# Seven products in two widths, and block sums from DRAM scratch, in three passes of a token-mixing MLP

## The chip, the cores and the metric

The kernel runs on one core of a Trainium2 chip. A core has a matrix engine (TensorE, in the profile PE, its weight loads PEld), a vector engine (VectorE, DVE), an activation engine (ScalarE, ACT), a general engine (GpSimd, POOL), and a sequencer that mostly issues DMAs (SyncE, SP). Sixteen DMA engines move data between DRAM and the core's memory (SBUF); matmul results lie in eight banks of PSUM. The metric is the device time in microseconds (us) of one execution, the median of several runs.

## The reference, cut to what matters

```python
h = x + A(layernorm(x))            # linear attention with softmax features, 32 heads
h2 = h + B(layernorm(h))           # token-mixing MLP

# B, with S = 2048 tokens, D = 512 channels, F = 1792 hidden units
u = einsum("bsd,sf->bdf", layernorm(h), w1) + b1
u = gelu(u)
y = einsum("bdf,fs->bds", u, w2) + b2
return y.transpose(0, 2, 1)
```

Everything is fp32. A matmul operand is split into a high part in the matrix engine's fast fp32 form and the rest, its low part; a product is then high x high + high x low + low x high, three matmuls.

## The kernel before

The core works through four stages. The projections of attention come first. Then come 18 turns (`for it in range(NT + 2)`, L840) of late attention: turn `it` transposes query features of token tile `it`, computes the attention output of tile `it - 1` on the matrix engine, adds the residual (`s_h`, L637), normalizes tile `it - 2` (`s_moments`, `s_rstd`, `s_hn`), and fills the matrix engine's remaining time with the first two of the MLP's seven passes over `w1` (`fill`, L703). Third come the other five passes over `w1` (letters `KINDS = "vuuuv"`, steps 0 to 39, eight steps a pass), and last the 56 steps (8 x 7) over `w2`. `step(n)` (L1143) runs one step; in `w1` a step takes two token tiles, in a pass of two times 128 hidden units.

A pass marked `v` multiplies plainly. A pass marked `u` multiplies 2 x 2 blocks by seven products instead of eight (a Strassen-Winograd scheme): P1 to P7 (L983) each pair one of seven weight blocks with one of seven activation blocks of 256 columns. Four blocks of `w1` are loaded (index 1 to 4); of the seven weight blocks used, three are plain (2, 3, 4) and four are sums (0, 1, 5, 6). `w_sums` (L793) makes the sums with four VectorE additions per pair of steps: index 0 = 3 + 1, 5 = 0 + 2, 6 = 4 + 5, and last 1 = 1 + 2. `w_parts` (L807) then splits a step's seven blocks, high part on ScalarE (L66), low part on VectorE (L67). Steps over `w2` use the same scheme.

`narrow` (L985) is a product of three matmuls of 256 columns. `wide` (L991) puts the high and the low part of the activations side by side in one bank: one matmul of 512 columns (high weights times both) and one of 256 (low weights times high); the two halves of the bank are added later. Before the change the `u` passes use only `narrow` (`products`, L1009, four banks a pass, from `four_banks`, L1006: one pass takes four banks of pool `ps_b`, the next two of `ps_f` and two of `ps_q`), while the steps over `w2` (`wide_step`, L1041) already take P2 to P5 with `wide` and P1, P6, P7 with `narrow`, in six banks. After a `u` pass `firsts` and `u_out` (L1015, L1024) add the products to four blocks of u, on one ScalarE copy and five VectorE operations; two steps later comes the gelu.

Raw weights come by SP in groups of two steps: `load_raw(g)` (L762) issues two DMAs of 256 KB, into one half of one of two buffers that hold four steps each (`BLOCK`).

In late attention the MLP's weights for `fill` come by SP too (`stream`, L686, tile `wraw`), one or two DMAs of 256 KB a turn, issued behind the store of a finished h tile (`out<-h`, L642) and the load of a coming one (`h<-in_x`, L635). In the same turn ScalarE makes the high part (`his`, L677), then VectorE the low part (`flush`, L684, tile `whl`), and `fill` multiplies with them from the next turn on.

The order on PE, DVE, ACT, POOL and SP from the end of the projections on is the order of the code (a manual schedule); each engine runs its own queue in order and waits on semaphores. `later`, `at` and `PENDING` place work at a step number; `U_ADDS` gives the steps at which POOL issues accumulating DMAs (`nc.gpsimd.dma_start(..., accum_op=ALU.add)`, L951), which add one tile to another on the way. An accumulating DMA is always issued by POOL here (queue q0 in the profile), plain ones by SP (q1).

Of the kernel before, what the change touches and what calls it, by code (L numbers as in the profile page):

```python
# [9 lines left out]
F32 = mybir.dt.float32  # L10
# [7 lines left out]
P = 128  # L18
# [14 lines left out]
UR = 6  # L33
PLAIN = 2
KINDS = "vuuuv"
HD = D // 2
NP = NF // 2
WARM = 9
# [1 line left out]


@with_exitstack
def block_kernel(ctx: ExitStack, tc: tile.TileContext, x, xT, wT, phic, wo, w1, b1, w2, b2,
                 kvmask, ident_in, out):
    nc = tc.nc

# [56 lines left out]
    ps_k = a1.enter_context(tc.tile_pool(name="ps_k", bufs=2, space=PSUM))  # L103
    ps_v = a1.enter_context(tc.tile_pool(name="ps_v", bufs=2, space=PSUM))
    kvp = ps_kv.tile([P, 4, 64], F32, name="kvp")

    X, XH, EQ, PK, VS, SQ, PS, W = {}, {}, {}, {}, {}, {}, {}, {}

# [373 lines left out]
    for j in range(KD):  # L482
        WO[j] = w2p.tile([P, D], F32, name=f"wo{j}")
        nc.sync.dma_start(WO[j], wo[j * P:(j + 1) * P, :])
    az = aq.enter_context(tc.tile_pool(name="az", bufs=2, side="right", reuse_waits="tile"))
    EZ = {}

# [305 lines left out]
    def w_sums(g):  # L793

        if 2 * g >= len(STEPS) or STEPS[2 * g][0] == "v":
            return
        plain = STEPS[2 * g][0] == "y"
        raw = BLOCK[g // 2 % 2] if plain else RAW[g]
        added = ADDED(2 * g)
        if not added:  # L800
            nc.vector.tensor_add(raw[:, :, 0], raw[:, :, 3], raw[:, :, 1])
        nc.vector.tensor_add(raw[:, :, 5], raw[:, :, 0], raw[:, :, 2])
        nc.vector.tensor_add(raw[:, :, 6], raw[:, :, 4], raw[:, :, 5])
        if not added:
            nc.vector.tensor_add(raw[:, :, 1], raw[:, :, 1], raw[:, :, 2])  # L805

    def w_parts(n):  # L807
        if n >= len(STEPS):
            return
        if n >= Y0 and (n - Y0) % 6 < 3:  # L810
            PARTS[n] = [big.tile([P, 7, P], F32R, name="wp", tag="big") for _ in range(2)]
        else:
            t = ws[n % 3].tile([P, 2, 7, P], F32R, name="wp")
            PARTS[n] = t[:, 0], t[:, 1]
        k = slice(1, 5) if STEPS[n][0] == "v" else slice(0, 7)
        split(PARTS[n][0][:, k], PARTS[n][1][:, k], RAW[n // 2][:, n % 2, k], nc.vector)

    CB_FIRST = (0, 1, 2, 3)
    U_ADDS = {0: (5, 7, 9), 1: (6, 8, 10), 2: (11, 13, 15), 3: (19, 21, 23), 4: (28, 30, 32), 5: (34, 35.5, 37)}
    HELD = (44,)  # L820
    T_WORK = {5: 39.5}
    U_WORK = {0: 26, 1: 28, 2: 30, 3: 32, 4: 34, 5: 38, 6: 41}
# [13 lines left out]
        return (ws[3] if j in CB_FIRST else cbb if j == 4 else hp).tile([P, 4, 2, HD], F32R, name=f"cb{j}")  # L836

    NB, DQ, DL = {}, [], []

    for it in range(NT + 2):  # L840
        if it < NT:
# [67 lines left out]
                DQ.extend(h_ops(j, nc.vector))  # L909
        if it in (14, 15):  # L910
            add_raw(it - 14)
        if it == 16:
            DQ.extend(h_ops(6, nc.vector))
    some(DL)
# [88 lines left out]
    def new_bank(pool):  # L1003
        return pool.tile([P, 2, HD], F32, name="py", tag="pu")

    def four_banks(i):  # L1006
        return [new_bank(q) for q in ((ps_b,) * 4, (ps_f, ps_f, ps_q, ps_q))[i]]

    def products(n, banks, x, first, last):  # L1009
        a, b, c, d = banks  # L1010
        for o, m, opens in ((a[:, 0], P1, True), (a[:, 1], P6, False), (d[:, 0], P7, True), (b[:, 0], P5, True),
                            (b[:, 1], P4, False), (c[:, 0], P3, True), (c[:, 1], P2, False)):
            narrow(o, n, m, x(m[1]), first and opens, last)

    def firsts(banks):  # L1015
        a, b, c, d = banks
        tmp = wqp.tile([P, 4, HD], F32, name="tmp", tag="small")
        nc.scalar.activation(tmp[:, 1], a[:, 0], AF.Copy)
        nc.vector.tensor_sub(tmp[:, 2], a[:, 1], tmp[:, 1])
        nc.vector.tensor_sub(tmp[:, 3], tmp[:, 2], d[:, 0])  # L1020
        nc.vector.scalar_tensor_tensor(tmp[:, 0], b[:, 0], -1.0, tmp[:, 2], op0=ALU.mult, op1=ALU.subtract)
        return tmp[:, 0:2], tmp[:, 3].unsqueeze(1).to_broadcast([P, 2, HD])

    def u_out(p, banks):  # L1024
        e, u3 = firsts(banks)
        U[p] = o = ur.tile([P, 4, HD], F32, name="u")
        nc.vector.tensor_add(o[:, 0:2], banks[1], u3)
        nc.vector.tensor_add(o[:, 2:4], banks[2], e)

    def u_gelu(p):  # L1030
        for i in range(2):
# [111 lines left out]
    def step(n):  # L1143

        kind, i, j = STEPS[n]
        if kind == "u":
            if j == 0:
                BANKS[0] = four_banks(i % 2)
            products(n, BANKS[0], lambda m: NB[j][m], j == 0, j == NT // 2 - 1)
            if j == NT // 2 - 1:  # L1150
                b = list(BANKS[0])
                later(0, lambda: u_out(i, b))
                later(2, lambda: u_gelu(i))
        elif kind == "v":
            if j == 0:
                PU[i] = [ps_b.tile([P, D], F32, name="pu", tag="pu") for _ in range(2)]
            wh_, wl_ = PARTS[n]
            for k in range(2):
                for c in range(2):
                    m, t = 1 + 2 * k + c, 2 * j + k  # L1160
                    mm3(PU[i][c], wh_[:, m], wl_[:, m], HN[t][:, 0], HN[t][:, 1], t == 0, t == NT - 1)
            if j == NT // 2 - 1:
                for c in range(2):
                    (later(0, lambda c=c: gelu(2 * i + c, PU[i][c])) if i < NP - 1 else gelu(2 * i + c, PU[i][c]))
        else:
            o = (last_step if i == NT // 2 - 1 else wide_step)(n, i, j)
            STORES.extend(o)
# [48 lines left out]
    def prepare(m):  # L1216

        if m >= len(STEPS):
            return
        w_parts(m)  # L1220
        made.add(m)
        if m >= Y0:
            if m % 4 == 2 and m > Y0 + 3:
                w_sums(m // 4 * 2 + 2)
        elif m % 2 == 0 and m + 2 < Y0:
            w_sums(m // 2 + 1)
        if m ^ 1 in made:
            load_raw(m // 2 + 4)
            add_raw(m // 2 + 3)
# [24 lines left out]
def _layout(A_x, A_wqkv, A_w_phi, A_wo, B_w1, B_b1, B_w2, B_b2):  # L1254
# [7 lines left out]
    for a in range(P // DH):  # L1262
# [9 lines left out]
        "phic": phic,  # L1272
        "wo": wo,
        "w1": np.asarray(B_w1),
        "b1": np.asarray(B_b1).reshape(NF, P).T,
        "w2": np.asarray(B_w2),
        "b2": np.asarray(B_b2).reshape(NT, P).T,
# [21 lines left out]
```

## Time and profile before

| what | value |
|---|---|
| time, median of 3 runs | 515.59 us (514.91 to 516.23) |
| span of the profiled execution | 513.1 us |
| granted TensorE clock | 1.000 |
| PE, DVE, ACT, POOL busy | 507.8, 438.4, 310.6, 261.1 us |
| turns of late attention | about 138 to 262 us of the span |
| the three `u` passes | 288.6 to 349.1 us |
| steps over `w2` | from 371.6 us |

The profiled execution has no time of its own beside its span; the median of the runs stands 2.5 us over that span, for what lies before the first and after the last instruction. A row of a timeline gives start and length in us, engine, line, operation, what it writes and reads, shapes and count, and in brackets how long the engine sat idle before it and what ended that. A group row gives count, busy time in us and the mean of one in ns.

### The profile page before, as it was taken

The page shows a single profiled execution, that of the slowest core. Times are in us where ns is not written, and L with a number is a line of the kernel's source. Part 1 is how long each engine was busy: PE and PEld are TensorE (multiplying, and loading weights), DVE is VectorE, ACT ScalarE, POOL GpSimd, SP SyncE. Part 2 cuts the span into 40 slices and gives each one's busy share as a digit, 9 for nine tenths or more (in the row PEclk, how much of TensorE's full clock was granted, in tenths as well). Part 3 has the DMA queues.
Part 4 walks back from the last instruction along what each step waited for, and adds up shares of the span by engine and source line. Part 5 has one row for each costly group of instructions (what it writes and reads, how often), then busy time and mean ns, then how long its engine had stood idle before and what let it go on. Part 6 is the DMA issues. An engine that isn't in the chain of part 4 may idle for free.

```text
span 513.1 us, 10496 instructions
## 1 busy us (share of the span) xinstructions
PE 507.8 (99%) x4024; PEld 441.7 (86%) x4024; DVE 438.4 (85%) x746; ACT 310.6 (61%) x557; POOL 261.1 (51%) x212
## 2 busy tenths in 40 slices
PE   8999999999999999999999999999999999999997
PEld 8888888888877777777788999998899999999997
DVE  6799889989887899699877898898799889868983
ACT  6999863525267878867676754577655444434530
POOL 3579997876999999985200421202323212211220
PEclk9999999999999999999999999999999999999999
DMA  8642301010123234354325775545677797668734
GB/s 308 217 144 84 103 22 42 1 65 21 42 64 103 67 100 145 127 169 132 95 69 185 150 159 125 133 115 151 173 164 147 181 199 167 122 153 190 169 51 85
DMA packets 53266, 63.35 MB, mean 123 GB/s; under 512 B 4832, under 2 KB 39904, under 8 KB 53216
## 3 DMA queue, kind: packets, MB, share of 16 engines
q1 hardware_dynamic: 44288, 51.90, 32.5%
q0 software_dynamic: 8640, 10.62, 14.9%
q8 instruction: 31, 0.51, 0.4%
q10 hardware_dynamic: 288, 0.17, 0.1%
q14 instruction: 19, 0.16, 0.1%
HBM read 48.39 MB, written 11.14 MB: 116 GB/s over the span
## 4 chain that ended last, share of the span: by engine, by line
PE 95%; DVE 2%; ACT 1%; DMA 1%; issue 0%; POOL 0%; DVEq 0%
PE py L989 25%; PE py L996 9%; PE pu L71 9%; PE pu L72 8%; PE pu L73 8%; PE py L998 4%; PE pk_ps L71 3%; PE pk_ps L72 3%; PE pk_ps L73 3%; PE pv L73 3%; PE pv L71 3%; PE pv L72 3%; PE po L71 3%; PE po L73 2%; PE po L72 2%; PE pn L616 2%
## 5 line engine op out<-in xcount | busy, mean ns | idle before, releaser
L66 ACT ACTIVATE wp<-wraw 128x896 fp32r<-128x896 f32 (+1 forms) x96 | 82.4, 895 | 68.3 <-DVE wraw L805 23.9
L67 DVE TENSOR_TENSOR wp<-wraw,wp 128x896 fp32r<-128x896 f32 (+1 forms) x96 | 95.5, 1019 | 14.9 <-ACT wp L66 14.6
L989 PE MATMUL py<-cb,wp 128*128 128x256 f32 x678 | 92.6, 283 | 0.0
L989 PEld LDWEIGHTS py<-cb,wp 128*128 128x128 f32 x678 | 86.1, 191 | 0.0
L1039 POOL DMA_DIRECT2D out<-u x28 | 24.8, 963 | 89.8 <-ACT u L1085 28.9
L951 POOL DMA_DIRECT2D tt<-u x14 | 13.4, 960 | 60.6 <-ACT tt L950 34.5
L490 POOL TENSOR_TENSOR ez<-eq,zB 128x1024 f32<-128x1024 f32 x16 | 38.4, 2406 | 3.8 <-ACT zB L550 3.8
L219 POOL TENSOR_TENSOR pk<-pk,sk 128x1024 f32<-128x1024 f32 x16 | 31.1, 1947 | 11.3 <-DVE sk L218 10.1
L996 PE MATMUL py<-cb,wp 128*128 128x512 f32 x126 | 36.1, 394 | 0.0
L514 POOL TENSOR_TENSOR eq<-eq,w 128x1024 f32<-128x1024 f32 x16 | 32.4, 2025 | 3.5 <-DVE w L511 3.5
L223 POOL TENSOR_TENSOR zacc<-zacc,pk 128x1024 f32<-128x1024 f32 x13 | 31.4, 2412 | 0.5
L989 PE MATMUL py<-hs,wp 128*128 128x256 f32 x216 | 30.0, 283 | 0.0
L989 PEld LDWEIGHTS py<-hs,wp 128*128 128x128 f32 x216 | 27.8, 192 | 0.1
L195 ACT ACTIVATE pk<-pk,r 128x1024 f32<-128x1024 f32 x16 | 18.4, 1149 | 15.0 <-DVE pk L173 14.4
L989 PE MATMUL py<-uf,wp 128*128 128x256 f32 x198 | 26.6, 283 | 0.0
L71 PE MATMUL pu<-wq,xs 128*128 128x512 f32 x64 | 26.1, 409 | 0.0
L71 PE MATMUL pu<-hs,whl 128*128 128x512 f32 x64 | 26.0, 406 | 0.0
L71 PE MATMUL po<-woh,oh 128*128 128x512 f32 x64 | 25.3, 396 | 0.1
L72 PE MATMUL pu<-wq,xs 128*128 128x512 f32 x64 | 25.0, 391 | 0.0
L73 PE MATMUL pu<-wq,xs 128*128 128x512 f32 x64 | 25.0, 390 | 0.0
L72 PE MATMUL pu<-hs,whl 128*128 128x512 f32 x64 | 25.0, 390 | 0.0
L73 PE MATMUL po<-woh,ol 128*128 128x512 f32 x64 | 25.0, 390 | 0.0
(226 smaller groups left out, 1422.1 us busy)
## 6 DMA issues: line engine op xcount, KB each, us to landing
wraw<-in_w SPq DMA_DIRECT2D x112, 256.0 KB, 3.4
out<-u POOLq DMA_DIRECT2D x21, 256.0 KB, 5.4
xraw<-in_xT SPq DMA_DIRECT2D x16, 256.0 KB, 2.9
xh<-in_x SPq DMA_DIRECT2D x16, 256.0 KB, 2.7
h<-in_x SPq DMA_DIRECT2D x16, 256.0 KB, 2.9
out<-h SPq DMA_DIRECT2D x16, 256.0 KB, 2.0
wraw<-in_wT SPq DMA_DIRECT2D x12, 256.0 KB, 4.9
tt<-u POOLq DMA_DIRECT2D x14, 128.0 KB, 3.8
```

What stands on the lines that cost most here:

```text
L66: nc.scalar.activation(hi, src, AF.Copy)
L67: lo_engine.tensor_sub(lo, src, hi)
L71: nc.tensor.matmul(o, ah, bh, start=first, stop=False)
L72: nc.tensor.matmul(o, ah, bl, start=False, stop=False)
L73: return nc.tensor.matmul(o, al, bh, start=False, stop=last).ins
L219: nc.gpsimd.tensor_mul(heads(PK[t]), heads(PK[t]), sk.unsqueeze(2).to_broadcast([P, 2 * H, DH]))
L223: nc.gpsimd.tensor_add(zacc, zacc, PK[t])
L490: nc.gpsimd.tensor_mul(EZ[t], EQ[t], zB)
L514: nc.gpsimd.tensor_mul(heads(EQ[t]), heads(EQ[t]), W[t].rearrange("p g c h -> p (g c h)").unsqueeze(2).to_broadcast([P, 2 * H, DH]))
L989: nc.tensor.matmul(o, w[:, m[0]], x[:, y], start=opens and i == 0, stop=closes and i == 2, skip_group_check=True)
L996: nc.tensor.matmul(o, wh_[:, m[0]], x(m[1]), start=first, stop=False, skip_group_check=True)
L1039: nc.gpsimd.dma_start(out[t * P:(t + 1) * P, k * HD:], flat(a), accum_op=ALU.add)
```

## The change

The three `u` passes now take their products as the steps over `w2` do: P1, P6, P7 with `narrow`, P2 to P5 with `wide` (P3, P2 first in a pass's first step and last in its last one), in six banks: four of `ps_b` in every pass, and two of `ps_f` or `ps_q` in turn. `u_out` adds the two halves of the four wide banks: five ScalarE copies and nine VectorE operations a pass.

Two of the four sums of weight blocks (index 0 and 1) no longer come from VectorE. The host lays the `u` passes' columns of `w1` out again as `w1u`, four planes of blocks for each pass (a copy in another order, no arithmetic). Six tensors of 512 KB in DRAM, `ZS[p][0]` and `ZS[p][1]` for the passes p = 3, 4, 5, are filled in two moves: SP copies a plane into each, DRAM to DRAM, right after the loads of `wo` (`sum_copy`), and POOL adds another plane with an accumulating DMA, DRAM to DRAM (`sum_add`), two at the end of each of the turns 11, 13 and 14 (`SUM_TURNS`). `load_raw` then takes a group of a `u` pass in three DMAs: three planes from `w1u` (384 KB) and 128 KB from each scratch tensor. `w_sums` makes the other two sums with two VectorE additions over four steps at a time.

```diff
+    ZS = {p: [dram.tile([P, NT // 2 * P], F32, name=f"zs{p}_{k}") for k in range(2)] for p in US}
+    def rows(a):
+        return a.rearrange("(a b) s -> a (b s)", b=2)
+    def sum_copy(p, k):
+        nc.sync.dma_start(rows(ZS[p][k]), rows(w1u[US.index(p), (2, 0)[k]]))
+    def sum_add(p, k):
+        nc.gpsimd.dma_start(rows(ZS[p][k]), rows(w1u[US.index(p), k]), accum_op=ALU.add, max_dma_last_dim=8192)
...
         nc.sync.dma_start(WO[j], wo[j * P:(j + 1) * P, :])
+    for p in US:
+        for k in range(2):
+            sum_copy(p, k)
...
+        kind, i, j = STEPS[2 * g]
+        if kind == "u":
+            RAW[g] = RAW[g].rearrange("p n m s -> p (n m s)").rearrange("p (m n s) -> p m n s", m=7, n=2)
+            cols = slice(j * P, j * P + 2 * P)
+            nc.sync.dma_start(RAW[g][:, 2:5].rearrange("p m n s -> p m (n s)"),
+                              w1u[US.index(i), 1:4, :, cols].rearrange("m p s -> p m s"))
+            for k in range(2):
+                nc.sync.dma_start(RAW[g][:, k].rearrange("p n s -> p (n s)"), ZS[i][k][:, cols])
+            return
...
+        raw = BLOCK[g // 2 % 2]
+        if STEPS[2 * g][0] == "u":
+            v = raw.rearrange("p (g n) m s -> p g (n m s)", g=2).rearrange("p g (m s) -> p g m s", m=7)
+            nc.vector.tensor_add(v[:, :, 5], v[:, :, 0], v[:, :, 2])
+            nc.vector.tensor_add(v[:, :, 6], v[:, :, 4], v[:, :, 5])
+            return
...
-    U_ADDS = {... 3: (19, 21, 23), ...}
+    U_ADDS = {... 3: (19, 21, 24), ...}
+    SUM_TURNS = (11, 13, 14)
+    def block_sums(it):
+        if it in SUM_TURNS:
+            for k in range(2):
+                sum_add(US[SUM_TURNS.index(it)], k)
...
+        if last:
+            singles()
+            wide(n, x, first, last, w5, w4)
+            wide(n, x, first, last, w3, w2)
+        elif first:
+            wide(n, x, first, last, w3, w2)
+            singles()
+            wide(n, x, first, last, w5, w4)
+        else:
+            wide(n, x, first, last, w3, w2, w5, w4)
+            singles()
+    def u_out(p, banks):
+        b16, b7, b5, b4, b3, b2 = banks
+        tmp = wqp.tile([P, 4, HD], F32, name="tmp", tag="small")
+        u3, e0, e1, u2 = [tmp[:, k] for k in range(4)]
+        U[p] = o = ur.tile([P, 4, HD], F32, name="u")
+        nc.scalar.activation(e1, b16[:, 0], AF.Copy)
+        for k, b in enumerate((b5, b4, b3, b2)):
+            nc.scalar.activation(o[:, k], b[:, 1], AF.Copy)
+        sub(u2, b16[:, 1], e1)
+        sub(u3, u2, b7[:, 0])
+        add(o[:, 0], b5[:, 0], o[:, 0])
+        add(o[:, 1], b4[:, 0], o[:, 1])
+        nc.vector.scalar_tensor_tensor(e0, o[:, 0], -1.0, u2, op0=ALU.mult, op1=ALU.subtract)
+        add(o[:, 0], o[:, 0], u3)
+        add(o[:, 2], b3[:, 0], o[:, 2])
+        add(o[:, 3], b2[:, 0], o[:, 3])
+        add(o[:, 1:4], o[:, 1:4], tmp[:, 0:3])
...
-                BANKS[0] = four_banks(i % 2)
+                BANKS[0] = six_banks((ps_f, ps_q)[i % 2])
...
-        elif m % 2 == 0 and m + 2 < Y0:
+        elif m % 4 == 2 and m + 2 < Y0:
             w_sums(m // 2 + 1)
```

Up to the end of the projections the order on every engine is the same as before. On PE, the first steps of the first `u` pass read before the change (`cb` and `hs` are activation blocks, `wp` a step's weight parts):

```order
L989 MATMUL py<-hs,wp 128x256 x3
L989 MATMUL py<-cb_3447,wp 128x256 x12
L989 MATMUL py<-hs,wp 128x256 x9
L989 MATMUL py<-cb_3448,wp 128x256 x12
L989 MATMUL py<-hs,wp 128x256 x9
```

and now, for the first step and the second:

```order
L1034 MATMUL py<-hs,wp 128x512 x2
L1036 MATMUL py<-hs,wp 128x256 x2
L1027 MATMUL py<-hs,wp 128x256 x3
L1027 MATMUL py<-cb_3467,wp 128x256 x6
L1034 MATMUL py<-cb_3467,wp 128x512 x2
L1036 MATMUL py<-cb_3467,wp 128x256 x2
L1034 MATMUL py<-hs,wp 128x512 x2
L1034 MATMUL py<-cb_3468,wp 128x512 x2
L1036 MATMUL py<-hs,wp 128x256 x2
L1036 MATMUL py<-cb_3468,wp 128x256 x2
L1027 MATMUL py<-hs,wp 128x256 x3
L1027 MATMUL py<-cb_3468,wp 128x256 x6
```

So 21 matmuls of 256 columns in a step become 13 of 256 and four of 512.

On POOL, at the end of late attention, the queue before holds these rows from turn 11 to turn 15 (`ez` and `eq` are tile products of attention, `r` is a tile's reciprocal deviation, `hs` the low part of a normalized tile):

```order
L67 TENSOR_TENSOR hs<-u,hs 128x512
L514 TENSOR_TENSOR eq<-eq,w 128x1024
L652 TENSOR_TENSOR r_69<-ve_3086,mhalf 128x1
L67 TENSOR_TENSOR hs<-u,hs 128x512
L514 TENSOR_TENSOR eq<-eq,w 128x1024
L652 TENSOR_TENSOR r_69<-ve_3184,mhalf 128x1
L67 TENSOR_TENSOR hs<-hf,hs 128x512
L652 TENSOR_TENSOR r_69<-ve_3278,mhalf 128x1
```

and now, from turn 12's end on:

```order
L68 TENSOR_TENSOR hs<-u,hs 128x512
L530 TENSOR_TENSOR eq<-eq,w 128x1024
L668 TENSOR_TENSOR r_69<-ve_3102,mhalf 128x1
L68 TENSOR_TENSOR hs<-u,hs 128x512
L118 DMA zs_0_118<-in_w1u 64x2048
L118 DMA zs_1_119<-in_w1u 64x2048
L530 TENSOR_TENSOR eq<-eq,w 128x1024
L668 TENSOR_TENSOR r_69<-ve_3200,mhalf 128x1
L68 TENSOR_TENSOR hs<-hf,hs 128x512
L118 DMA zs_0_120<-in_w1u 64x2048
L118 DMA zs_1_121<-in_w1u 64x2048
L668 TENSOR_TENSOR r_69<-ve_3296,mhalf 128x1
```

Two accumulating DMAs of 64 rows of 2048 words now stand behind the low part of a tile and ahead of the next turn's work, here in turns 13 and 14; the pair of turn 11 stands the same way.

On SP, after the projections, the queue before goes from the loads of `wo` to the turns' loads of x (`h`), stores of h and loads of weights (`wraw`):

```order
L484 DMA wo_1393<-in_wo 128x512
L484 DMA wo_1395<-in_wo 128x512
L635 DMA h<-in_x 128x512 x2
L642 DMA out<-h 128x512
L691 DMA wraw<-in_w 128x2x256
```

and now:

```order
L497 DMA wo_1401<-in_wo 128x512
L497 DMA wo_1403<-in_wo 128x512
L115 DMA zs_0_116<-in_w1u 16x8192
L115 DMA zs_1_117<-in_w1u 16x8192
L115 DMA zs_0_118<-in_w1u 16x8192
L115 DMA zs_1_119<-in_w1u 16x8192
L115 DMA zs_0_120<-in_w1u 16x8192
L115 DMA zs_1_121<-in_w1u 16x8192
L651 DMA h<-in_x 128x512 x2
```

The six copies stand between the last load of `wo` and the first load of a turn.

More of the change, by code (lines that the diff above doesn't have):

```diff
@@ L35 @@
 KINDS = "vuuuv"
+US = [p for p, k in enumerate(KINDS, PLAIN) if k == "u"]
 HD = D // 2
@@ L1004, in new_bank, with six_banks @@
         return pool.tile([P, 2, HD], F32, name="py", tag="pu")
-    def four_banks(i):
-        return [new_bank(q) for q in ((ps_b,) * 4, (ps_f, ps_f, ps_q, ps_q))[i]]
+    def six_banks(pool):
+        b3, b2 = [new_bank(pool) for _ in range(2)]
+        return [new_bank(ps_b) for _ in range(4)] + [b3, b2]
     def products(n, banks, x, first, last):
[L1010 to L1013, printed above, removed]
@@ new lines, in singles @@
+        def singles():
+            narrow(b16[:, 0], n, P1, x(P1[1]), first, last)
+            narrow(b16[:, 1], n, P6, x(P6[1]), False, last)
+            narrow(b7[:, 0], n, P7, x(P7[1]), first, last)
+        w3, w2, w5, w4 = (b3, P3), (b2, P2), (b5, P5), (b4, P4)
+        if last:
[9 more added lines that the diff above has]
+            singles()
```

26 lines of the change are left out of this document (10 added, 16 removed).

## The prediction

> **What bounds the kernel now.** I read the page first: its busy times and its chain of waits.
>
> ```profile
> span 513.1 us, 10496 instructions
> PE 507.8 (99%) x4024; PEld 441.7 (86%) x4024; DVE 438.4 (85%) x746; ACT 310.6 (61%) x557; POOL 261.1 (51%) x212
> PE 95%; DVE 2%; ACT 1%; DMA 1%; issue 0%; POOL 0%; DVEq 0%
> ```
>
> PE is busy for 507.8 of 513.1 us and holds 95% of the chain that ended last. So there are only two currencies here: PE work taken away shortens the run by its own length, and each new PE wait lengthens it by its own. The median of the runs, 515.59, stands 2.5 us over this span; I keep that distance and work on the span.
>
> Next the chain in order of time, for the stage that changes and for the steps over `w2`, which already run the new form.
>
> ```profile
> 288.63 60.47 PE py L989 x504
> ...
> 371.58 1.08 PE py L989 x9
> ...
> 374.75 1.08 PE py L989 x9
> 375.82 0.93 PE py L996 x4
> 376.75 0.47 PE py L998 x4
> ...
> 388.89 1.07 PE py L989 x9
> ```
>
> The three `u` passes are one unbroken run of 504 matmuls, 60.47 / 504 = 0.120 us each, 24 steps of 2.520 us. In a step over `w2`, nine narrow matmuls take 1.08 (0.120 each), four of 512 columns 0.93 (0.232 each), four of 256 columns 0.47 (0.118 each).
>
> **The products.** Both forms stream the same columns: a narrow product 3 x 256, a wide one 512 + 256. Only the small surplus of a matmul over its columns is saved, four times a step. From 371.58 to 388.89 lie seven steps over `w2`, a change of passes among them: 17.31 / 7 = 2.473 us. A step gains 2.520 - 2.473 = 0.047, and 24 steps gain **1.1 us**. That is all PE can win: 0.2%. What a measurement of this kernel tells from no change is about 0.3%, 1.55 us, so even the undisturbed change would stay inside it.
>
> **VectorE and ScalarE in the passes.** The window over the first `u` pass, and VectorE's groups in the passes over `w1`:
>
> ```profile
> 288.63:308.79 20.16, 20.16 (x171) 20.16 (x170) 19.27 (x34) 12.87 (x21) 7.56 (x9) 1.00 0.76 163
> ...
> L802 DVE TENSOR_TENSOR wraw<-wraw 128x256 f32<-128x256 f32 x12 | 5.1, 426 | 0.4
> L67 DVE TENSOR_TENSOR cb<-tt,cb 128x768 fp32r<-128x768 f32 x3 | 2.8, 950 | 0.0
> L1027 DVE TENSOR_TENSOR u<-py,tmp 128x512 f32<-128x512 f32 x3 | 2.0, 680 | 0.0
> L801 DVE TENSOR_TENSOR wraw<-wraw 128x512 f32<-128x512 f32 x2 | 1.4, 690 | 0.0
> ```
>
> The columns after the window's length are PE, PEld, DVE, ACT, POOL. VectorE is busy for 19.3 of 20.2 us. Eight additions of 256 columns per four steps (8 x 0.42 = 3.4) become two of 512 (1.4): 4 us less in a pass. `u_out` grows from three operations of 256 and two of 512 columns (3 x 0.42 + 2 x 0.68 = 2.6) to eight of 256 and one of 768, an estimate of 8 x 0.42 + 0.95 = 4.3 with the 768-column row beside it at 0.95. Net VectorE wins about 2.3 us a pass. ScalarE gets four more copies of 256 columns, some 1.5 us (0.36 each, the row below), with 7 us free. PE never waits for either here, so this saves nothing and costs nothing.
>
> **Banks.** Each `u` pass now takes the four `ps_b` banks that the pass before used. The tightest place is the end of the last `u` pass, where the plain pass opens with its first matmul in the bank of P1 and P6:
>
> ```profile
> 347.46 0.36 ACT L1018 ACTIVATE tmp<-py 128x256 f32<-128x256 f32 x1
> 348.33 0.42 DVE L1019 TENSOR_TENSOR tmp<-py,tmp 128x256 f32<-128x256 f32 x1
> 348.94 0.40 PE L71 MATMUL pu<-hs,wp 128*128 128x512 f32 x1
> ```
>
> The copy and the subtraction that free that bank end at 348.75, 0.2 us ahead of that matmul, and P1 and P6 still come early in a last step (1.4 us before its end). Between two `u` passes 0.7 us of P3 and P2, in other banks, come first. I take 0; 0.5 us a boundary, three boundaries, is the bound if VectorE runs late.
>
> **The copies.** SP issues them behind the `wo` loads and ahead of the turns:
>
> ```profile
> 111.46 1.75 SPq L484 DMA_DIRECT2D wo<-in_wo  x4
> 138.02 0.81 SPq L635 DMA_DIRECT2D h<-in_x  x2
> q1 hardware_dynamic: 44288, 51.90, 32.5%
> ```
>
> Queue q1 cost 0.325 x 513.1 / 51.90 = 3.2 us of all sixteen engines per MB, so 3.15 MB take 10 us, or 20 as an upper estimate since both ends lie in DRAM, in 25 us in which SP issues nothing. I take 0.
>
> **The additions, POOL's side.** These rows surround the three places (the low part `hs`, then the next turn's `eq` or `r`, with its wait):
>
> ```profile
> 221.33 1.29 POOL L67 TENSOR_TENSOR hs<-u,hs 128x512 fp32r<-128x512 f32 x1 [0.48 <-ACT hs L66]
> 224.69 1.94 POOL L514 TENSOR_TENSOR eq<-eq,w 128x1024 f32<-128x1024 f32 x1 [2.06 <-DVE w L511]
> ...
> 238.29 1.29 POOL L67 TENSOR_TENSOR hs<-u,hs 128x512 fp32r<-128x512 f32 x1 [3.74 <-ACT hs L66]
> 240.07 1.94 POOL L514 TENSOR_TENSOR eq<-eq,w 128x1024 f32<-128x1024 f32 x1 [0.48 <-DVE w L511]
> ...
> 248.89 0.65 POOL L652 TENSOR_TENSOR r<-ve,mhalf 128x1 f32<-128x1 f32 x1 [2.39 <-ACT ve L649]
> ...
> 417.00 0.86 POOL L1039 DMA_DIRECT2D out<-u  x1 [5.89 <-ACT wp L66]
> ```
>
> Two issues, 0.86 each by the last row, fit the 2.06 us before 224.69 and the 2.39 before 248.89. Before 240.07 only 0.48 is free, so `eq` and then `r` come 1.3 us later; PE wants that `eq` a turn later. I take 0, at most 0.3.
>
> **The additions, the DMA engines' side.** This is the dearest part. The weights that `fill` multiplies are loaded in the same turns, and used soon. The rows of turn 14 to 15, from the issue of a load to PE:
>
> ```profile
> 241.43 0.45 SPq L691 DMA_DIRECT2D wraw<-in_w  x1
> wraw<-in_w SPq DMA_DIRECT2D x1, 256.0 KB, 3.0
> 245.05 0.61 ACT L677 ACTIVATE whl<-wraw 128x512 fp32r<-128x512 f32 x1
> 247.32 0.68 DVE L684 TENSOR_TENSOR whl<-wraw,whl 128x512 fp32r<-128x512 f32 x1
> 249.51 0.68 DVE L625 TENSOR_TENSOR ol<-pn,oh 128x512 fp32r<-128x512 f32 x1
> 250.65 0.40 PE L71 MATMUL po<-woh,oh 128*128 128x512 f32 x1
> ```
>
> The load lands 3.0 us after its issue, at 244.4. VectorE makes the low part at 247.32, and in its queue the `ol` that PE's `po` matmuls need stands 2.2 us behind; it ends at 250.2, 0.45 us before PE uses it. So the load may land at 247.32 + 0.4 - 0.65 = 247.1 at the latest; beyond that PE waits one for one.
>
> How long do two additions of 0.524 MB hold the engines, and does a load wait for them? No addition from DRAM to DRAM is in the trace. The nearest rows are the accumulating stores in the `w2` stage, windows 412 to 417 and 340 to 350 (queue rows), and two loads there: one issued at 409.0 with the queue empty, one at 410.05, behind two accumulating stores of 0.262 MB (2 x 256 KB) issued at 409.3 and 409.9:
>
> ```profile
> q0 software_dynamic: 265, 0.48, 54.6%
> q0 software_dynamic: 288, 0.26, 16.9%
> wraw<-in_w SPq DMA_DIRECT2D x1, 256.0 KB, 2.7
> wraw<-in_w SPq DMA_DIRECT2D x1, 256.0 KB, 5.1
> ```
>
> The price is 0.546 x 5 / 0.48 = 5.7 us of all engines per MB with pieces of 2 KB, 0.169 x 10 / 0.26 = 6.5 with pieces of 1 KB. 0.524 MB of additions, 3.0 us of work, delayed the load by 5.1 - 2.7 = 2.4, that is 0.8 of the work: plain loads do not slip past. The pair of a turn is 1.05 MB; 5.7 us per MB makes 6.0 us (5.0 if the 8 KB pieces are cheaper still, 7.5 by the whole q0 row). Issued at 239.6, it is in full course when the load of 241.43 comes: 244.4 + 0.8 x 6.0 = 249.2, which is **2.1 us** too late (1.3 to 3.3). I take 2.1.
>
> In turns 11 and 12 the additions start at 222.6, the two loads at 226.06, when a third of the work is done:
>
> ```profile
> wraw<-in_w SPq DMA_DIRECT2D x2, 256.0 KB, 4.8
> 230.86 1.28 ACT L677 ACTIVATE whl<-wraw 128x512 fp32r<-128x512 f32 x2 [1.14 <-DMA wraw<-in_w]
> 234.86 0.60 ACT L620 ACTIVATE oh<-pn 128x512 fp32r<-128x512 f32 x1 [1.28 <-PE pn L616]
> ```
>
> ScalarE waited 1.14 us for them already, but 1.28 idle us and some 0.6 more up to PE lie behind. A further delay of up to 0.8 x 4 = 3.2, partly taken up by the idle engines in the 4.8, leaves between 0 and 1.4 us; I take **0.3**. In turn 15 the loads are late again, but the whole chain is already 2 us later by then: 0.
>
> **The sum.** 513.1 - 1.1 + 2.1 + 0.3 = 514.4 of span, and 2.5 around it: **516.9 us**, 0.25% slower, inside what counts as no change.
>
> [...]
>
> **Rivals.**
>
> *The cover holds.* The additions cost about what q1 costs, 3.2 us per MB, 3.4 us a turn: the load lands at 244.4 + 0.8 x 3.4 = 247.1, just in time, and the loads of turn 12 too. Then 513.1 - 1.1 + 2.5 = 514.5 us. For it: the pieces are large, and the lateness begins only beyond 2.7 us. Against it: both rows of q0.
>
> *The additions are bound by DRAM, and the run is slower.* They read two streams and write one, all in DRAM; q0's rows above have at least one side in the core. The most the page shows is 308 GB/s, in the first slice:
>
> ```profile
> GB/s 308 217 144 84 103 22 42 1 65 21 42 64 103 67 100 145 127 169 132 95 69 185 150 159 125 133 115 151 173 164 147 181 199 167 122 153 190 169 51 85
> ```
>
> 3 x 1.05 MB / 308 GB/s = 10.2 us a turn. The load of 241.43 lands at 244.4 + 0.8 x 10.2 = 252.6, 5.5 us late, those of turn 12 up to 4 us late: 513.1 - 1.1 + 9.5 + 2.5 = 524.0. It decides from about 6.3 us of work a turn, where PE loses 2.65 us and the run is slower by 0.3%.
>
> *The banks are late.* 0.5 us at three boundaries on top of the sum: 518.4. Against it, the seven steps at 2.473 with a change of passes among them.
>
> **How the numbers follow.** Additions of 5.0 to 7.5 us a turn that delay loads (515.5 to 518.7): 0.50, of which 0.28 lies below 517.14, the 0.3% line. The cover holds (514.0 to 515.5): 0.28, of which 0.05 falls under 514.04, 0.3% faster, by the scatter of the runs (514.91 to 516.23). Additions longer than 7.5 us: 0.15. Banks: 0.07. So slower 0.22 + 0.15 + 0.07 = 0.44, faster 0.05, same 0.51; the time forecast is the likeliest case's, 516.9. The range from 514.3 to 520.5 leaves out about a tenth above (the DRAM-bound case) and somewhat less below.
>
> **What would show it.** In the profile after: narrow and wide matmuls in the `u` passes at 0.120, 0.232 and 0.118, steps at 2.473 and no PE idle at the four pass boundaries; the landing of the load issued near 241 at 7 to 8 us instead of 3.0; VectorE idle before the low part of `whl` there, ended by ScalarE, and PE idle before a `po` of turn 15, ended by `ol`; q0 larger by 3.15 MB and its price per MB. It would be wrong if that load lands within 5.6 us (cover), if PE's waits in turns 12 to 16 add to more than 3.5 us, or if the waits lie in the `u` passes instead.

## The result and the profile after

The changed kernel takes **524.86 us** (median of 4 runs, 523.25 to 525.27) against 515.47 for the kernel before beside it (4 runs): a ratio of **1.0176**, 95% interval 1.0163 to 1.0189. It is slower by 9.4 us; the prediction was 516.9, with a range up to 520.5. The profiled execution spans 523.4 us against 513.1.

First the same three rows of the page, of the changed kernel, and then its chain of `u` steps:

```profile
span 523.4 us, 10330 instructions
PE 510.0 (97%) x3928; PEld 437.5 (84%) x3928; DVE 433.2 (83%) x722; ACT 313.4 (60%) x569; POOL 265.8 (51%) x218
PE 81%; DMA 6%; DVE 5%; issue 3%; ACT 3%; POOL 1%; SPq 0%; POOLq 0%; DVEq 0%; ACTq 0%
```
```profile
322.20 1.07 PE py L1027 x9
323.28 0.93 PE py L1034 x4
324.21 0.47 PE py L1036 x4
...
332.10 1.07 PE py L1027 x9
```

The products are as forecast: four steps in 9.90 us, 2.475 each, of 1.07, 0.93 and 0.47. But PE's share of the chain has gone from 95% to 81%, and DMA, VectorE, ScalarE and issue hold what it lost. PE's own waits, in total, times and longest, say where (before, nothing above 1.1 us stood in this view, and none of these four rows):

```profile
PE po L72 <- DVE ol L641: 3.7, 4, 1.6
PE py L1027 <- DVE tmp L1078: 2.3, 1, 2.3
PE pu L72 <- ACT whl L693: 1.5, 1, 1.5
PE py L1027 <- DVE u L1136: 1.1, 1, 1.1
```

The 5.2 us of `po` and `pu` lie in turns 12 to 16; 2.3 at the change from the first `u` pass to the second; 1.1 at a change of passes over `w2`.

**The loads in turns 13 to 16.** In order of time, from the additions to PE (all engines of the changed kernel):

```profile
241.44 1.64 POOL L118 DMA_DIRECT2D zs<-in_w1u  x2
243.43 0.66 SPq L707 DMA_DIRECT2D wraw<-in_w  x1
252.67 0.63 ACT L693 ACTIVATE whl<-wraw 128x512 fp32r<-128x512 f32 x1 [4.81 <-DMA wraw<-in_w]
253.33 0.69 DVE L700 TENSOR_TENSOR whl<-wraw,whl 128x512 fp32r<-128x512 f32 x1 [3.04 <-ACT whl L693]
253.35 0.50 PE L72 MATMUL pu<-hs,whl 128*128 128x512 f32 x1 [1.47 <-ACT whl L693]
256.27 0.50 PE L72 MATMUL po<-woh,oh 128*128 128x512 f32 x1 [0.99 <-DVE ol L641]
...
261.30 0.63 ACT L693 ACTIVATE whl<-wraw 128x512 fp32r<-128x512 f32 x1 [3.58 <-DMA wraw<-in_w]
264.47 0.50 PE L72 MATMUL po<-woh,oh 128*128 128x512 f32 x1 [1.62 <-DVE ol L641]
```

ScalarE stands 4.81 us before a load; the high part, VectorE's low part and the `ol` behind it come late in turn. And the same happens again a turn later, 8.6 us on. The median landing times of the loads at 243.4 and 251.2, and what the additions' queue took of the engines from 241.5 to 251:

```profile
wraw<-in_w SPq DMA_DIRECT2D x1, 256.0 KB, 9.2
...
wraw<-in_w SPq DMA_DIRECT2D x1, 256.0 KB, 10.1
...
q0 software_dynamic: 161, 1.06, 64.4%
```

The two loads took 3.0 and 4.8 us before. The additions' work is 0.644 x 9.5 = 6.1 us, and the load of 243.43 lands 9.2 - 3.0 = 6.2 us later than before, as much as all of that work. The load of 251.19 lands 10.1 - 4.8 = 5.3 us later, 0.9 of it. A load without additions in front varies too: near 241 it landed after 3.0 us before the change and after 4.4 in the profiled execution of no_adds below, where SP spent 1.89 us on its issue instead of 0.45. So 0.8 of the work or all of it can't be told apart from one load.

**VectorE beside GpSimd.** A second thing in turn 13, with no load in it (the first row is the kernel before, the others the changed kernel):

```profile
240.45 2.10 DVE L684 TENSOR_TENSOR whl<-wraw,whl 128x512 fp32r<-128x512 f32 x1
...
242.45 3.16 DVE L700 TENSOR_TENSOR whl<-wraw,whl 128x512 fp32r<-128x512 f32 x1
242.56 2.49 POOL L530 TENSOR_TENSOR eq<-eq,w 128x1024 f32<-128x1024 f32 x1
245.53 0.68 DVE L641 TENSOR_TENSOR ol<-pn,oh 128x512 fp32r<-128x512 f32 x1
246.26 0.50 PE L72 MATMUL po<-woh,oh 128*128 128x512 f32 x1 [0.69 <-DVE ol L641]
```

An operation that takes 0.69 us at 253.33 takes 3.16 here. It ends 0.56 after GpSimd's `eq`. Before the change it stood beside `eq` as well, took 2.10 and ended 0.54 after it (242.55 and 242.01); with the two issues ahead of it `eq` starts 0.11 us after the low part instead of 0.38 before it (240.07), and its row is 0.55 us longer (2.49 instead of 1.94). So 1.1 us of this are the change's, and PE waits 0.69 where it did not wait before. Why it ends behind `eq` both times, no run shows.

**The change of `u` passes.** ScalarE's queue, VectorE and PE at step 16:

```profile
317.58 0.42 ACT L988 ACTIVATE tt<-tt 128x256 f32<-128x256 f32 x1 [3.18 <-DMA tt<-u]
317.90 0.37 ACT L1075 ACTIVATE tmp<-py 128x256 f32<-128x256 f32 x1
318.30 0.42 DVE L1078 TENSOR_TENSOR tmp<-py,tmp 128x256 f32<-128x256 f32 x1 [2.78 <-ACT tmp L1075]
318.77 0.62 PE L1027 MATMUL py<-hs,wp 128*128 128x256 f32 x3 [2.26 <-DVE tmp L1078]
```

The first copy of `u_out` (L1075) would free the bank of P1 and P6 but stands in ScalarE's queue behind a copy of `u_adds` (L988) that waits 3.18 us for an accumulating DMA. Before, the same two copies stood in the same order; the first did not have to wait there, and the next pass had other banks, so nobody waited for the second.

Where the 10.3 us of the two spans lie, by three marks of PE: the first `pn` matmul of the turns, the first matmul of the `u` passes, the end of the last matmul (us; the experiments below are in it too):

| kernel | turns begin | turns to `u` | `u` to the end | median time |
|---|---|---|---|---|
| before | 142.2 | 146.3 | 221.2 | 515.4 to 515.6 |
| **after** | 143.0 | 152.9 | 224.2 | 524.86 |
| no_adds | 142.1 | 146.3 | 223.9 | 514.82 |
| eighth | 142.3 | 147.2 | 221.0 | 515.69 |
| plain_late | 142.3 | 147.9 | 222.3 | 517.25 |
| single | 142.7 | 150.3 | 220.4 | 518.16 |
| pieces_2k | 142.9 | 153.4 | 222.8 | 523.05 |
| u_add | 142.3 | 155.2 | 220.3 | 522.49 |
| early_adds | 142.1 | 158.8 | 220.7 | 528.13 |
| early_u | 142.3 | 158.9 | 220.1 | 527.14 |
| pre_adds | 154.5 | 146.3 | 220.1 | 527.25 |
| pre_adds_u | 152.4 | 146.3 | 223.6 | 526.14 |
| gap_adds | 142.4 | 146.8 | 221.4 | 515.61 |
| wide_only | 142.2 | 146.3 | 222.8 | 515.86 |

Of the 10.3, 6.6 lie in the turns, 3.0 behind them, and 0.8 ahead of them. That 0.8 is there before the first copy is issued, and kernels with the same program up to there begin the turns anywhere from 142.1 to 143.0, so it is the scatter of a start.

The listed waits are shorter than what they cost: 5.2 us in the turns against 6.6 lost, at a granted clock of 1.00 throughout. A wait is counted from the end of the last matmul, 0.40 us after its start, while back to back the next one starts after 0.23; and behind a wait the second matmul starts 0.34 after the first (256.27 and 256.61). That is 0.17 + 0.11 = 0.28 us more for a wait, 1.4 for the five. In the same way the two waits behind the turns, 3.3 us by the list, cost 224.2 - 220.3 = 3.9 against u_add, which has neither; u_add is 0.9 faster there than the kernel before.

### The profile page after: what moved, and what is told of

The parts are those of the page before. It is cut to its first block, busy times and chain, and to the rows that moved or that the text cites. A ratio compares the mean times of both kernels' runs of the same rounds, so it can differ in the third digit from the quotient of the medians.

```text
span 523.4 us, 10330 instructions
## 1 busy us (share of the span) xinstructions
PE 510.0 (97%) x3928; PEld 437.5 (84%) x3928; DVE 433.2 (83%) x722; ACT 313.4 (60%) x569; POOL 265.8 (51%) x218
## 3 DMA queue, kind: packets, MB, share of 16 engines
HBM read 56.25 MB, written 17.43 MB: 141 GB/s over the span
## 4 chain that ended last, share of the span: by engine, by line
PE 81%; DMA 6%; DVE 5%; issue 3%; ACT 3%; POOL 1%; SPq 0%; POOLq 0%; DVEq 0%; ACTq 0%
PE py L1027 17%; PE py L1034 11%; PE pu L72 7%; PE pu L73 6%; PE pu L74 6%; PE py L1036 6%; DMA wraw<-in_w 3%; PE pk_ps L72 3%; PE pk_ps L74 3%; PE pk_ps L73 3%; PE pv L74 3%; PE pv L72 3%; PE pv L73 3%; PE po L72 2%; PE po L74 2%
## 5 line engine op out<-in xcount | busy, mean ns | idle before, releaser
L1027 PE MATMUL py<-cb,wp 128*128 128x256 f32 x534 | 75.3, 283 | 1.1 <-DVE u L1136 1.1
L1027 PEld LDWEIGHTS py<-cb,wp 128*128 128x128 f32 x534 | 68.7, 190 | 1.3 <-DVE u L1136 1.3
L1034 PE MATMUL py<-cb,wp 128*128 128x512 f32 x174 | 51.2, 395 | 0.0
L1034 PEld LDWEIGHTS py<-cb,wp 128*128 128x128 f32 x174 | 29.7, 189 | 3.7
L1036 PEld LDWEIGHTS py<-cb,wp 128*128 128x128 f32 x174 | 28.5, 188 | 4.0
L1036 PE MATMUL py<-cb,wp 128*128 128x256 f32 x174 | 31.0, 279 | 0.0
L700 DVE TENSOR_TENSOR whl<-wraw,whl 128x512 fp32r<-128x512 f32 x16 | 19.3, 1204 | 8.5 <-ACT whl L693 8.5
L72 PE MATMUL pu<-wq,xs 128*128 128x512 f32 x64 | 26.1, 409 | 0.0
L74 PE MATMUL pu<-wq,xs 128*128 128x512 f32 x64 | 25.0, 390 | 0.0
```

The lines of the kernel that those rows point to most:

```text
L72: nc.tensor.matmul(o, ah, bh, start=first, stop=False)
L74: return nc.tensor.matmul(o, al, bh, start=False, stop=last).ins
L1027: nc.tensor.matmul(o, w[:, m[0]], x[:, y], start=opens and i == 0, stop=closes and i == 2, skip_group_check=True)
L1034: nc.tensor.matmul(o, wh_[:, m[0]], x(m[1]), start=first, stop=False, skip_group_check=True)
L1036: nc.tensor.matmul(o[:, 0], wl_[:, m[0]], x(m[1])[:, 0], start=False, stop=last, skip_group_check=True)
```

## The experiments

**No additions (no_adds).** The core of the edit:

```diff
     def block_sums(it):
-        if it in SUM_TURNS:
-            for k in range(2):
-                sum_add(US[SUM_TURNS.index(it)], k)
+        pass
```

> The changed kernel without its six additions in DRAM (the scratch keeps the copied planes alone, so the second term of block sums 0 and 1 of the u passes is left out). Theory: the loads of the turns stand behind the additions in the DMA engines, and all of the 6.6 us that the turns lost is theirs: the load issued near 243 lands in 3.0 us again, no PE wait on ol or whl in turns 11 to 16, and the run takes 524.9 - 6.6 = 518.3 us. Rival one: the wait at the change of u passes (2.3 us, step 15 to 16) is only the echo of late turns; then it goes too: 516.0. Rival two: the copies or the new order are at fault, not the additions: above 522.

Measured: 514.82 us (10 runs, 513.99 to 518.7), ratio to before 0.9992 (0.997 to 1.0014). The additions cost 10.0 us (524.86 - 514.82). The turns take 146.3 us as before, so the copies and the new order cost nothing there. Rival one comes nearest: most of the wait at step 16 goes too. Not always: the profiled execution, 517.4 us, still has it,

```profile
PE py L1025 <- DVE tmp L1076: 2.0, 1, 2.0
```

while spans of 512.2 to 513.8 in most others leave no room for it.

**The wait at step 16 (u_add).**

```diff
-    U_ADDS = {..., 2: (11, 13, 15), 3: (19, 21, 24), ...}
+    U_ADDS = {..., 2: (11, 13, 15.5), 3: (19, 21, 24), ...}
```

> The changed kernel with the third additions of the plain pass's column (U_ADDS[2]) at 15.5 instead of 15, so that in ScalarE's queue u_out's copies stand ahead of the copy that waits for an accumulating DMA. Theory: the 2.3 us that PE waits at step 16 are ScalarE's wait for that DMA and go in full: 524.9 - 2.3 = 522.6. Rival: the banks themselves come late (eight operations of VectorE in u_out), half of it stays: 523.8 or more.

Measured: 522.49 (521.92 to 523.89), 2.4 us less than the changed kernel. ScalarE's queue there now:

```profile
315.90 0.36 ACT L1075 ACTIVATE tmp<-py 128x256 f32<-128x256 f32 x1
316.64 1.35 ACT L1077 ACTIVATE u<-py 128x256 f32<-128x256 f32 x4 [0.38 <-PE py L1036]
318.61 0.42 ACT L988 ACTIVATE tt<-tt 128x256 f32<-128x256 f32 x1 [0.61 <-DMA tt<-u]
```

The copies go first, the other one waits behind them, and PE waits nowhere in the passes: from `u` to the end it takes 220.3 us, 0.9 less than before. (Its turns took 2.3 us longer than those of the changed kernel in the profiled execution: one wait for `ol` was 3.0 us there, and a granted clock of 0.50 from 266 to 268 followed it.) The theory holds: the wait was the queue in front of `u_out`, not VectorE's eight operations.

**Additions in early turns (early_adds, early_u).** One a turn in turns 2 to 7; early_u has U_ADDS at 15.5 besides.

```diff
-    SUM_TURNS = (11, 13, 14)
+    SUM_TURNS = (2, 3, 4, 5, 6, 7)
...
-            for k in range(2):
-                sum_add(US[SUM_TURNS.index(it)], k)
+            sum_add(US[SUM_TURNS.index(it) // 2], SUM_TURNS.index(it) % 2)
```

> The changed kernel with its additions one a turn in turns 2 to 7, where the DMA engines are idle most of a turn, instead of two in turns 11, 13 and 14. Theory: what cost 6.6 us is the meeting of two additions with a load that has 2.7 us to spare; one addition (half of the work, 3 to 4 us) delays a load by less than that: 518.3, and 516.0 if the wait at step 16 is an echo. Rival: any addition stalls the loads beside it by more than their slack: 521 or more.

> Both edits: additions one a turn in turns 2 to 7, and U_ADDS[2] third at 15.5. If the two losses are independent: 524.9 - 6.6 - 2.3 = 516.0. If what is left is the gain of PE alone, 515.5 - 1.1 = 514.4, the wait at the step over w2 (1.1 us) must have been an echo as well. If losses reappear elsewhere, 518 or more.

Measured: 528.13 (526.85 to 529.43) and 527.14 (526.3 to 528.44). The time is the rival's, its reason is not: no load of `wraw` took more than 4.9 us to land (5.3 in no_adds), but in these turns GpSimd has no room. Before the change it was busy 77.1 of the 79 us from 143 to 222 already. Its rows, and VectorE, PE and the granted clock (the seventh number, behind POOL) of early_adds:

```profile
187.91 1.51 POOL L68 TENSOR_TENSOR hs<-u,hs 128x512 fp32r<-128x512 f32 x1
189.14 1.09 POOL L118 DMA_DIRECT2D zs<-in_w1u  x1
189.76 2.44 POOL L530 TENSOR_TENSOR eq<-eq,w 128x1024 f32<-128x1024 f32 x1
191.65 1.06 POOL L668 TENSOR_TENSOR r<-ve,mhalf 128x1 f32<-128x1 f32 x1
192.19 2.83 POOL L506 TENSOR_TENSOR ez<-eq,zB 128x1024 f32<-128x1024 f32 x1
194.63 1.60 POOL L68 TENSOR_TENSOR hs<-u,hs 128x512 fp32r<-128x512 f32 x1
...
188.24 8.55 DVE L700 TENSOR_TENSOR whl<-wraw,whl 128x512 fp32r<-128x512 f32 x1 [1.33 <-ACT whl L693]
...
198.04 0.79 PE L72 MATMUL po<-woh,oh 128*128 128x512 f32 x1 [8.08 <-DVE ol L641]
```
```profile
200.00:202.00 2.00, 2.00 (x6) 1.56 (x5) 1.02 (x4) 0.00 (x0) 0.78 (x1) 0.50 0.79 164
```

GpSimd runs without a pause, VectorE's low part takes 8.55 us beside it, where the one at 204.12, with GpSimd idle, takes 0.69, and PE waits 8.08 for the `ol` behind it. Then it runs at a granted clock of 0.50: twelve `po` matmuls 0.43 us apart where 0.23 is usual, 2.4 us more. So the additions need room on GpSimd as much as in the DMA engines.

**An eighth of the additions, and plain copies (eighth, plain_late).** Both issue six instructions at the places of the change.

```diff
# eighth
-        nc.gpsimd.dma_start(rows(ZS[p][k]), rows(w1u[US.index(p), k]), accum_op=ALU.add, max_dma_last_dim=8192)
+        nc.gpsimd.dma_start(rows(ZS[p][k])[0:8], rows(w1u[US.index(p), k])[0:8], accum_op=ALU.add, max_dma_last_dim=8192)
# plain_late
+        nc.gpsimd.dma_start(rows(ZS[p][k]), rows(w1u[US.index(p), k]), max_dma_last_dim=8192)
```

> The changed kernel with each of the six additions cut to its first eighth (64 KB instead of 512; seven eighths of the second term of block sums 0 and 1 are left out). GpSimd issues the same six instructions at the same places. Theory: the loss is the load that stands behind 1 MB of additions; with an eighth of it the delay is below 1 us, inside the 2.7 us that the load may be late, and the loss goes but for the VectorE operation that GpSimd's shifted work holds up (a PE gap of about 1 us in turn 13): 515 to 516.5. Rival: the issue on GpSimd and what it holds up on VectorE is the larger part: 520 or more.

> The changed kernel with the six additions as plain copies from DRAM to DRAM, on the same queue, in the same pieces of 8 KB, at the same places (the scratch then holds planes 0 and 1 alone, so one term of block sums 0 and 1 is left out). The bytes written are the same, a third of the traffic (the read of the old value) is gone. If what costs is the read, add and write of an accumulating piece, the load of 243 lands in 5 us or less and the time is 515 to 518. If the bytes that stand in the queue cost, however they are moved: 520 to 525, the load at 7 us or more.

Measured: eighth 515.69 (10 runs, 515.14 to 519.43; 1.0013, 0.9994 to 1.0032), plain_late 517.25 (10 runs, 515.58 to 521.67; 1.0046, 1.0015 to 1.0077). The theory of eighth holds. Its turns are 147.2 us against 146.3 in no_adds, so the bare issue, with what it moves on VectorE (3.23 us for the same low part), is worth 0.9 us; the two medians alone could not tell that. Seven eighths of the data are worth 524.86 - 515.69 = 9.2. In plain_late the time is where the theory put it and the load is not, as the rows below show; four of its ten runs took 520.3 to 521.7, as the rival had it. In its profiled execution the queue's row from 240 to 250 and the loads in it read

```profile
q0 software_dynamic: 216, 1.51, 49.6%
...
wraw<-in_w SPq DMA_DIRECT2D x2, 256.0 KB, 6.7
```

that is 0.496 x 10 / 1.51 = 3.3 us per MB, against 0.644 x 9.5 / 1.06 = 5.8 for the additions. A pair of copies is 3.4 us of work. The load of 241.59 took 6.6 us and that of 248.90 took 6.7, against 3.0 and 4.8 before: 3.6 and 1.9 later, more than the theory's 5 us of landing and less than the rival's 7. The first is little over the 2.7 us of margin, and the turns lose 1.6 us instead of 6.6. An addition made a byte 1.8 times as dear as a copy, and the part over the margin many times. Not all of what the turns gain is the DMA engines': two plain issues hold GpSimd for 1.10 us instead of 1.64.

**One a turn (single).**

```diff
-    SUM_TURNS = (11, 13, 14)
+    SUM_TURNS = (11, 12, 13, 14, 15, 16)
...
-            for k in range(2):
-                sum_add(US[SUM_TURNS.index(it)], k)
+            sum_add(US[SUM_TURNS.index(it) // 2], SUM_TURNS.index(it) % 2)
```

> The changed kernel with one addition a turn in turns 11 to 16 instead of two in turns 11, 13 and 14. The same work in DMA and on GpSimd, in halves of 3 us. Theory of the margin: a load may be 2.7 us late, so 3 us of work cost a turn at most 0.5: 516 to 517.5. Rival: the work counts, not its division (a turn that is late by less is late more often): 521 or more.

Measured: 518.16 (3 runs, 517.44 to 518.56; 1.0051, 1.0035 to 1.0066), between the two and nearer the theory: half the work at a time costs 4.0 us in the turns instead of 6.6. A fourth run took 526.77 at a granted clock of 0.992; its reason stays open. That it cost more than the theory gives begins with the load issued at 241.95, 1.9 us behind one addition, which lands in

```profile
wraw<-in_w SPq DMA_DIRECT2D x1, 256.0 KB, 7.2
```

us instead of 3.0: 4.2 us for 0.524 x 5.8 = 3.0 of work. The loads of 233.60, 248.99 and 257.35 landed 3.0, 2.3 and 2.4 us later than their like before (6.1, 7.1 and 5.3 against 3.1, 4.8 and 2.9), so one of four lost more than the work. And the largest wait is one that I had not counted, behind the load of turn 16:

```profile
PE pu L73 <- DVE hs L682: 1.6, 1, 1.6
```

**Pieces of 2 KB (pieces_2k).** `max_dma_last_dim=2048` for 8192 in `sum_add`.

> The changed kernel with the additions in pieces of 2 KB instead of 8 KB. By the windows the price of an accumulated MB was 5.7 us in pieces of 2 KB (stores of the w2 stage) and is 5.1 to 5.8 in pieces of 8 KB: 524 to 526, no difference. [...]

Measured: 523.05 (2 runs, 521.86 and 524.23). Its row from 241.5 to 251:

```profile
q0 software_dynamic: 487, 0.96, 64.4%
```

0.644 x 9.5 / 0.96 = 6.4 us per MB against 5.8: the larger pieces are cheaper by a tenth, and the two runs do not show it in the time.

**Before the turns (pre_adds, pre_adds_u, gap_adds).** In pre_adds three additions stand ahead of the last tile's logits and three ahead of `s_ez(0)`, and the copies at the head of that hand-ordered part; pre_adds_u has U_ADDS at 15.5 besides.

> The full change with copies and additions moved ahead of the turns: the copies before the wo loads, three additions in each of two gaps of GpSimd (3.6 us idle before 114.8, 3.8 us before 127.0) where the DMA engines are busy 0.24 to 0.41. Theory: the loss belongs to the place, where neither GpSimd nor the DMA engines have room, not to the additions as such: 514.8, as without additions. Rival: the additions delay the wo loads or GpSimd's ez, which the turns cannot make up: 518 or more.

> As the run before, with the third additions of the plain pass's column at 15.5 instead of 15. The run without additions had a wait of 2.0 us at step 16 in its profiled execution (515.6 of span) and, by its spans of 512.2 to 513.8, none in most others. Theory: with the copy behind u_out the wait cannot come, 514.4 and no execution above 516. Rival: what waits is something else; then as the run before.

Measured: 527.25 (525.21 to 529.8) and 526.14 (523.96 to 527.55). They did not test what they were meant to: nothing held the copies back, and the scheduler put them and three additions 14 to 26 us into the program, into the first loads. PE stood 5 us there, and the turns of pre_adds began 12 us late:

```profile
PE pk_ps L74 <- POOL xs L68: 4.8, 1, 4.8
```

After that pre_adds has 146.3 and 220.1 in the table, as good as any. pre_adds_u waited nowhere at step 16, as its theory had it, but 2.3 us at a change of passes over `w2`. So gap_adds keeps the copies where the change has them and puts all six additions into one gap of GpSimd:

```diff
     v += 1
+    for k in range(6):
+        sum_add(US[k // 2], k % 2)
     s_ez(0)
...
-    U_ADDS = {..., 2: (11, 13, 15), 3: (19, 21, 24), ...}
+    U_ADDS = {..., 2: (11, 13, 15.5), 3: (19, 21, 24), ...}
```

> The full change, copies where they were, all six additions in GpSimd's idle 3.8 us ahead of the turns (at 123 us, before ez), and U_ADDS[2] third at 15.5. The run before with early copies lost its time in the first 50 us, where its copies and three additions had gone, and nothing after them: 146.2 us of turns, 220.1 us from the first u step to the end. Theory: start of turns at 142.2, then the same two stretches: 508.5, with the 3.5 behind PE's last matmul 512.0 of span, 513.9 us. Rival: six issues take 5 us, GpSimd enters the turns 1.3 us late, and as with additions in turns 2 to 7 it never makes that up: 518 or more.

Measured: **515.61** (11 runs, 514.67 to 518.38), ratio to before 1.0003 (0.9988 to 1.0017). The same additions that cost 10.0 us in turns 11 to 14 cost 0.8 here, by medians whose intervals overlap, and with u_add's edit beside them. The six issues and the `ez` behind them:

```profile
123.15 5.01 POOL L118 DMA_DIRECT2D zs<-in_w1u  x6
127.02 5.92 POOL L506 TENSOR_TENSOR ez<-eq,zB 128x1024 f32<-128x1024 f32 x2
```

GpSimd ran 1.2 us late into the turns, and they took 0.5 us more (146.8 against 146.3). The forecast of 513.9 was 1.7 us too good: in the profiled execution 0.6 in the turns and 1.3 behind them against the 146.2 and 220.1 that it went by, where PE waited 0.4 once at a change of passes over `w2`; the rest is not placed.

**The wide products alone (wide_only).** The kernel before with the new `products`, `six_banks` and `u_out`, its four VectorE sums, no scratch, and U_ADDS as in gap_adds.

> The kernel before with the wide products, the six banks and the new u_out alone; all four block sums stay on VectorE, no DRAM scratch, U_ADDS[2] third at 15.5. PE gains its 1.1 us. Theory: VectorE was busy 19.3 of 20.2 us in a u pass and gets 1.7 more, so it becomes the bound by some 0.8 us a pass: 515.4 - 1.1 + 2.4 = 516.7. Rival: it has slack at the ends of the passes and PE's gain comes through: 514.4.

Measured: 515.86 (10 runs, 515.29 to 516.47; 1.0003, 0.9988 to 1.0019), between the two. Two waits take back what PE gains:

```profile
PE pu L71 <- DVE tmp L1040: 0.9, 1, 0.9
PE py L989 <- DVE u L1098: 0.6, 1, 0.6
```

The first is the end of the last `u` pass, the place that the prediction named as the tightest. That the scratch took something off VectorE that mattered is not shown: no_adds, which differs by it and by U_ADDS, is 1.0 us faster, but the two intervals overlap (0.997 to 1.0014 and 0.9988 to 1.0019). No version here beats the kernel before by more than the runs can tell.

## Why the prediction was wrong

By its own steps:

- *The products, -1.1.* Right. Steps of 2.475 us, and from `u` to the end 220.1 us in pre_adds and early_u, which waited nowhere there, 1.1 less than before.
- *The copies, 0.* Right: no_adds has them.
- *The additions' work, 6.0 us a turn.* Right: 6.1. The delay of a load as 0.8 of the work was low in turn 13, 1.0 (6.2 of 6.1), and nearly right a turn later, 0.9; over all the loads above it lies between 0.6 and 1.4. (Of the two rows of q0 that gave the price, the one with 6.5 us per MB, window 340 to 350, holds additions between tiles in the `u` passes and not stores of the `w2` stage.)
- *The load of turn 13, +2.1 (1.3 to 3.3).* Right in mechanism and nearly in size: 1.47 + 0.99 us of waits, 3.0 with the 0.28 that each costs beside, by the path that was described. *The loads of turn 12, +0.3:* 0.44 of wait, 0.7 in all.
- *"In turn 15 the loads are late again, but the whole chain is already 2 us later by then: 0."* **This is the step that failed first.** The additions are issued within the chain and move with it, so the later start gives no margin. The pair of turn 14 is issued 1.1 us later into the turns than in eighth (249.35 - 143.0 against 247.60 - 142.3), the load of 251.19 took 10.1 us, and PE waited 1.62 us in the next turn, 1.9 in all.
- *GpSimd's side, 0, at most 0.3.* Too low. I asked what `eq` makes late, and not how long VectorE's low part gets beside GpSimd's moved work (3.16 us instead of 2.10): 0.69 us of wait in turn 13, 1.0 in all, and 0.9 by eighth.
- *Banks, 0, at most 0.5 a boundary.* **This is the second.** I priced the two operations that free the bank, at the boundary into the plain pass, and not what stands ahead of them in ScalarE's queue. There a copy that waits for a DMA was harmless as long as nobody waited for the one behind it. That cost 2.3 us of wait, 2.5 in all, at the boundary from the first `u` pass to the second; none was lost at the one that I named.
- *PE waits one for one.* Not quite: each listed wait cost 0.28 us more than its length, and in other runs a long one was followed by a granted clock of 0.50 (8.08 us in early_adds, 3.0 in u_add).

The terms of the turns come to +2.4 in the prediction and 6.6 in the run (0.7 + 1.0 + 3.0 + 1.9); the boundary adds 2.5. The wait of 1.1 over `w2` comes and goes between kernels that differ in nothing there (0.4 in gap_adds, none in u_add, 2.3 in pre_adds_u), so I do not put it to the change. The 2.5 us that the sum adds to the span were 0.6 too many: the profiled run of the changed kernel took 525.27 us for its 523.4 of span, 1.9 more.

Of the rivals, *the additions are bound by DRAM* gave 524.0 and is nearest in time, but its price is refuted: it took 10.2 us of work for a pair, and a pair was 6.1 in turn 13. In gap_adds six additions issued together land 2.46 us apart (130.96, 133.42, 135.88 and so on), 4.9 us a pair, less than half of what the 308 GB/s gave. The third stream of that price, the read of the old value, stands in no count: the changed kernel's page has 3.15 MB more read than that of no_adds (56.25 against 53.10) and 3.14 more written (17.43 against 14.29), the bytes of the six additions once each. Whether DRAM bounds at a higher rate was not tested. *The cover holds*, 514.5, is what happens without the additions' data (514.8), or with them in another place (515.6).

What stays open: why one load was delayed by more than the work in front of it, and why the DMA before step 16 was late. Its landing took 4.97 us in the changed kernel, 5.35 in pieces_2k and 4.98 in the profiled execution of no_adds, but 2.96 before and 3.88 in eighth.

## What to carry to other kernels

A transfer that is moved into the background is priced in two currencies at once: what it keeps from the DMA engines, about all of which a load issued right behind it waits (here 1.0 and 0.9 of it, in turns 13 and 14), and what its issuing engine then does at another time. Look at each place where it meets a load with a margin, and let every later place start from the same margin, since work issued in a chain moves with the chain.

When an edit makes an engine wait for an operation that nobody waited for before, read the whole queue ahead of that operation; a wait on a DMA in it becomes yours (here 3.18 us of ScalarE, 2.26 of PE).

And where the sure gain is 0.2%, ask first whether a simpler form reaches it: here waits of 0.4 to 2.0 us at three places (step 16, the end of the last `u` pass, a change of passes over `w2`) took back most of it in one version or another.

## What was unexpected in the hardware

- An accumulating copy from DRAM to DRAM took 2.46 us per 0.524 MB in a row (gap_adds; 4.7 us per MB), 5.8 beside other transfers (the changed kernel); a plain copy on the same queue 3.3 (plain_late).
- A VectorE operation with two SBUF inputs took 8.55 us beside five GpSimd operations in a row with a DMA issue among them (early_adds), and ended 0.56 after the fifth; the same operation took 0.69 at 204.12 with GpSimd idle.
- After a wait of 8.08 us in early_adds PE ran twelve matmuls in 5.2 us, at a granted clock of 0.50 from 198 to 202 and of 0.68 in the next 2 us. After waits of about 2 us the clock was 0.50 in no_adds (2.0 of wait, then 0.50 from 312 to 314) and not in the changed kernel (2.26 of wait, 1.00 from 318 to 322):

```profile
312.00:314.00 2.00, 2.00 (x9) 1.80 (x9) 1.93 (x6) 0.48 (x1) 0.00 (x0) 0.50 0.44 73
```
```profile
318.00:320.00 2.00, 1.23 (x10) 1.23 (x11) 1.60 (x5) 2.00 (x6) 0.89 (x1) 1.00 0.61 192
```

So the length of a wait alone does not tell whether a lower clock follows it: the shorter of these two had it. What decides it, no run here shows.
